# A fused state-space layer, forward and backward: long-convolution transforms in two matmul stages with a block transpose by VectorE, with their tables kept on chip

## The chip, the cores and the metric

The kernel runs on one core of a Trainium2 chip. The metric is the device time in microseconds (us) of one execution. A matmul engine (PE), a vector engine (DVE), an activation engine (ACT), a general engine (POOL) and a queueing engine (SP) run their own instruction streams, in order, and meet through semaphores; sixteen DMA engines move data between memory and the on-chip buffers. Matmul results land in PSUM, and from there ACT or DVE copies them to the ordinary on-chip memory (SBUF), where the next matmul can read them.

## The reference

Sizes are L = 2048 time steps, D = 512 channels, N = 128 states, F = 1792 hidden units, all in bf16.

```python
x  = A_u                                        # [1, L, D]
xn = layernorm(x)
# s = S4 convolution: a kernel K per channel, applied by FFT of length 2L
dt = exp(log_dt)[:, None]
P  = exp((dt * A)[:, :, None] * arange(L))      # A = A_re + i A_im, [D, N]
K  = einsum("dn,dnl,dn->dl", C, P, dt * B).real
s  = irfft(rfft(pad(xn.T, 2L)) * rfft(pad(K, 2L)))[:, :L].T + xn * Dskip
# gate
g  = silu(silu(xn @ w1) @ w2)
out = x + s * g
# result: out and the gradients of A_u, A_re, A_im, B_re, B_im, C_re, C_im,
#         log_dt, Dskip, w1, w2 for a given grad_out
```

The convolution needs a forward transform of xn, of K and of the gradient of s (called DS in the kernel), three products of spectra (xn with K for s; xn with DS for the gradient of K; K with DS for the gradient of xn) and three inverse transforms. Everything else is matrix products, the tables of powers that make K and take its gradient back, and elementwise work.

## The kernel before

Sequences of length 2048 lie in SBUF as 128 partitions by 16 tiles t by 512 channels; a transform runs over partitions and t. The program is written in six stages, with the order of all engines' instructions set by hand: generators that each yield after a piece of work are advanced against one another in loops.

**Stage 1** runs the layernorm, the FFN forward (`gen_ffn_fwd`, L554 to L639) and, between its pieces, two kinds of tables: the powers (`power_phases`) and the DFT tables (`dft_table_phases`, L375 to L431). The DFT table has 16 slices of 128 by 8 by 128. Nine are made by a fraction (`frac`, L271 and L272, DVE) and three passes of ACT (L399, L402, L403), seven more are mirrored from those by a matmul (L411) and an ACT copy (`tb_m`). Each slice is stored to memory in two forms, `TFd` for forward transforms and, transposed by PE or by the DMA (L420 to L427, copied at `tb_i`), `TId` for inverse ones.

**Stage 2** makes the convolution kernel K in four chunks (`chunk_tables` L807 makes table products on DVE, `chunk_K` L862 does the matmuls), transposes the power tables for later use (`gen_xt`, `gen_yt`: PE transposes, ACT copies L948 and L965, stores to `XTd` and `YTd`), and takes the spectrum of xn. The forward transform (`fwd_classes` L1004) is a dense matmul: the four residue classes of t each take 8 matmuls of 128x128x512 for a quarter kt of the spectrum, with a quarter of the table loaded from `TFd`; one ACT copy (L1013) for each class; then a radix-4 pass on DVE (`rad4`, L92 to L98: 2 full, 3 small and 2 full instructions). Spectra are stored to memory, `UXd` for xn. K itself is stored to `Kud` and loaded again in another order (`load_K`).

**Stage 3** (`gen_kt` L1244) takes K's spectrum in quarters (`fwd_eo`, matmuls at L1180, copies at L1182, with negated tables `TFn` made by ACT at L1145), stores it to `KXd`, multiplies it with xn's (`cplx_mul`, L106 to L109: two multiplications of 4096 elements a partition and two additions of 2048) and makes an inverse radix-4 pass.

**Stage 4** runs the inverse transform that gives s (`inv_mm` L1198; 16 matmuls of 128x128x512, L1204, for each pair of t, with table tiles `TIs` loaded from `TId`), scales it by ACT into `S_s` (L1455, two buffers), stores `S_s`, and makes the output gradient from it (`YOut`). Between the pairs stands the forward transform of DS (`DXform` L1390).

**Stage 5** runs the inverse transform for K's gradient dK, sums it in groups (L1639), stores the sums and loads them again as `Gt`; in its midst the products for the gradient of xn (`Prod` L1564). Then come the slabs (`Slabs` L1734), which take the gradient back through the power tables: for each step a product on DVE (`Gbd`, L1774), matmuls on quarter-width tiles (L1786), an ACT copy (`Vb`, L1788), products and sums on DVE (L1797 to L1800) and matmuls (L1815). Between slab steps stand the inverse transform for xn's gradient (`conv`, copied at L1700) and most of the gradient of w2 (`Dw2` L1594, 14 blocks of two halves, matmuls at L1611).

**Stage 6** is the backward FFN (L1872 to L1936), the gradients of w1 (L1996) and the last of the state-space parameters.

Of the kernel before, what the change touches and what calls it, by code (L numbers as in the profile page):

```python
# [14 lines left out]
P = 128  # L15
# [5 lines left out]
W = 512  # L21
TS = 2
# [65 lines left out]
def rad4(nc, out_e, out_o, A, t, inv):  # L88

    TT = nc.vector.tensor_tensor  # L90
    E, O = t[:, 0], t[:, 1]
    TT(out=t[:, :, :, 0, :].rearrange("p e c w -> p c e w"), in0=A[:, :, 0:2, :], in1=A[:, :, 2:4, :], op=ALU.add)  # L92
    TT(out=E[:, :, 1, :], in0=A[:, :, 0, :], in1=A[:, :, 2, :], op=ALU.subtract)
    i, j = (1, 3) if not inv else (3, 1)
    TT(out=O[:, 0, 1, :], in0=A[:, 1, i, :], in1=A[:, 1, j, :], op=ALU.subtract)
    TT(out=O[:, 1, 1, :], in0=A[:, 0, j, :], in1=A[:, 0, i, :], op=ALU.subtract)
    TT(out=out_e, in0=E, in1=O, op=ALU.add)
    TT(out=out_o, in0=E, in1=O, op=ALU.subtract)  # L98


def cplx_mul(nc, pool, a, b, conj_a=False):

    TT = nc.vector.tensor_tensor
    t1 = pool.tile([P, 2, 4, W], BF16, name="cm_t1", tag="cm_t1")
    t2 = pool.tile([P, 2, 4, W], BF16, name="cm_t2", tag="cm_t2")
    TT(out=t1[:], in0=b[:, :], in1=a[:, 0:1].to_broadcast([P, 2, 4, W]), op=ALU.mult)  # L106
    TT(out=t2[:], in0=b[:, :], in1=a[:, 1:2].to_broadcast([P, 2, 4, W]), op=ALU.mult)  # L107
    TT(out=t1[:, 0], in0=t1[:, 0], in1=t2[:, 1], op=ALU.add if conj_a else ALU.subtract)
    TT(out=t1[:, 1], in0=t1[:, 1], in1=t2[:, 0], op=ALU.subtract if conj_a else ALU.add)  # L109
    return t1  # L110
# [25 lines left out]
def kernel(ctx, tc, A_u, A_A_re, A_A_im, A_B_re, A_B_im, A_C_re, A_C_im, A_log_dt, A_Dskip, B_x, B_w1, B_w2, grad_out,  # L136
# [23 lines left out]
    k.TFd = dr.tile([4, P, T, 2, P], BF16, name="TFd")  # L160
    k.TId = dr.tile([P, T, 8, P], BF16, name="TId")
    XS = lambda nm: dr.tile([4, P, 2, 4, W], BF16, name=nm)
    k.UXd = XS("UXd"); k.DXd = XS("DXd"); k.KXd = XS("KXd")
# [6 lines left out]
    with tc.manual_schedule():  # L170
        stage_1(k)
        stage_3(k, *stage_2(k))
        stage_4(k)
        stage_5(k)
        stage_6(k)
# [198 lines left out]

def dft_table_phases(k, pool):  # L375

    nc = k.nc
    kv = pool.tile([P, 512], I32, name="kv", tag="tb_r")
    nc.gpsimd.iota(kv[:], pattern=[[4, 512]], base=1, channel_multiplier=0)
    kf = pool.tile([P, 512], F32, name="kf")  # L380
    nc.vector.tensor_copy(out=kf[:], in_=kv[:])
    lf = pool.tile([P, T], F32, name="lf")
    nc.vector.tensor_scalar(out=lf[:], in0=k.lvf[:], scalar1=1.0 / 8192.0, scalar2=None, op0=ALU.mult)
    nJ = pool.tile([P, P], BF16, name="nJ")
    nc.gpsimd.memset(nJ[:], 0.0)
    nc.gpsimd.affine_select(out=nJ[:], in_=nJ[:], compare_op=ALU.not_equal, fill=-1.0, base=1 - P, pattern=[[1, P]], channel_multiplier=1)
    st = {}
    nC = [0]

    def A(t):  # L390
        r = pool.tile([P, 512], I32, name="tb_r", tag="tb_r")
        v = pool.tile([P, 512], F32, name="tb_v", tag="tb_v", bufs=2)
        frac(nc, v[:], r[:], kf[:], lf[:, t:t + 1])
        st[t] = v

    def B(t):
        v = st[t]
        w = pool.tile([P, 512], F32, name="tb_w", tag="tb_w", bufs=2)
        nc.scalar.activation(out=w[:], in_=v[:], func=ACT.Abs)  # L399
        tf = pool.tile([P, 4, 2, P], BF16, name="tb_f", tag="tb_f", bufs=4)  # L400
        rr = lambda ap: ap.rearrange("p (a b) -> p a b", b=P)
        nc.scalar.activation(out=tf[:, :, 1, :], in_=rr(v[:]), func=ACT.Sin, scale=-2.0 * math.pi)  # L402
        nc.scalar.activation(out=tf[:, :, 0, :], in_=rr(w[:]), func=ACT.Sin, scale=-2.0 * math.pi, bias=k.halfpi[:])  # L403
        st[t] = tf

    def M(t):

        tf, tm = st[t], pool.tile([P, 4, 2, P], BF16, name="tb_m", tag="tb_f", bufs=4)
        ps = k.pd.tile([P, 2, 4, P], F32, name="ps_m", tag="pd")
        for c in range(2):  # L410
            nc.tensor.matmul(out=ps[:, c], lhsT=nJ[:], rhs=tf[:, :, 1 - c, :], start=True, stop=True)  # L411
        later(k, nc.scalar.copy, out=tm[:].rearrange("p a c b -> p c a b"), in_=ps[:])
        st[16 - t] = tm

    def C(t):
        tf = st[t]
        ti = pool.tile([P, 8, P], BF16, name="tb_i", tag="tb_i", bufs=2)
        nC[0] += 1
        if nC[0] % 2 == 0:
            nc.sync.dma_start_transpose(ti[:], tf[:].rearrange("p a c b -> p (a c b)"))  # L420
        nc.sync.dma_start(k.TFd[:, :, t].rearrange("a p c b -> p a c b"), tf[:])
        if nC[0] % 2:
            pt = k.ps.tile([P, 8, P], BF16, name="pt_ti", tag="pz", bufs=1)
            for i in range(8):
                nc.tensor.transpose(out=pt[:, i, :], in_=tf[:, i // 2, i % 2, :], identity=k.ident[:])
            later(k, nc.vector.tensor_copy, out=ti[:], in_=pt[:])
        st[t] = ti  # L427

    def S(t):
        nc.sync.dma_start(k.TId[:, t], st.pop(t)[:])  # L430
    return A, B, M, C, S  # L431
# [121 lines left out]
def gen_ffn_fwd(k, fs, W1, W2):  # L553
# [52 lines left out]
    for tc_ in range(4):  # L606
# [5 lines left out]
        for f0 in range(0, FT, 2):  # L612
# [13 lines left out]
            k.mid()  # L626
# [11 lines left out]
    for _ in prev:  # L638
        k.mid()  # L639
        yield  # L640


def ld_tf(k, kt, q=None):

    k.ntf += 1
    if k.ntf % 2:
        TFs = k.tfp.tile([P, DK, F], BF16, name="TFs", tag="W1")[:].rearrange("p k f -> p (k f)")[:, 0:T * 2 * P].rearrange("p (t c q) -> p t c q", t=T, c=2)
    else:
        TFs = k.tf2.tile([P, T, 2, P], BF16, name="TFs", tag="TFs")[:]
    (q or k.nc.sync).dma_start(TFs, k.TFd[kt])  # L650
    return TFs


def stage_1(k):
# [3 lines left out]
    k.ntf = 0  # L658
    k.tfp = ro.open("tfp"); fp = ro.open("fp"); fs = ro.open("fs", 2)
    pr = lo.open("pr")  # L660
    W1 = k.tfp.tile([P, DK, F], BF16, name="W1", tag="W1")
# [10 lines left out]
    tA, tB, tM, tC, tS = dft_table_phases(k, tab)  # L672
    s0, s1, s2, pX, pV, pA, pB, pC, pCC, pS = power_phases(k, pr, bs, k.par)
    at, mid, ready = {}, {}, []
# [88 lines left out]
def open_tables(k, b, q, fn=None):  # L763
# [480 lines left out]
def gen_kt(k, kq, K_b, UX):  # L1244
# [3 lines left out]
    st = {}  # L1248
# [792 lines left out]
```

## Time and profile before

| | us |
|---|---|
| runs shown (median) | 729.01 |
| lowest and highest of three | 724.71, 729.33 |
| span of the profiled execution | 724.9 |

The profiled execution's span lies at the low end of the runs, some 4 us under the median. A profile line gives the time of one execution: an engine's busy time, its share of the span and its number of instructions; in a table by stretches, each row is a stretch of the span with its length and each engine's busy time in it. The stage borders by the trace are about 155 to 168 (stage 1 ends), 288 (stage 3 begins), 413 (dK's inverse transform begins), 455 (it ends), 480 (first slab matmul) and 566 (stage 6 begins). The clock column is the granted clock of PE as a share of full speed. Line numbers such as L1204 are those of the kernel before.

### The profile page before, as it was taken

The page shows a single profiled execution, that of the slowest core. Times are in us where ns is not written, and L with a number is a line of the kernel's source. Part 1 is how long each engine was busy: PE and PEld are TensorE (multiplying, and loading weights), DVE is VectorE, ACT ScalarE, POOL GpSimd, SP SyncE. Part 2 cuts the span into 40 slices and gives each one's busy share as a digit, 9 for nine tenths or more (in the row PEclk, how much of TensorE's full clock was granted, in tenths as well). Part 3 has the DMA queues.
Part 4 walks back from the last instruction along what each step waited for, and adds up shares of the span by engine and source line. Part 5 has one row for each costly group of instructions (what it writes and reads, how often), then busy time and mean ns, then how long its engine had stood idle before and what let it go on. Part 6 is the DMA issues. An engine that isn't in the chain of part 4 may idle for free.

```text
span 724.9 us, 13172 instructions
## 1 busy us (share of the span) xinstructions
PE 643.6 (89%) x5068; PEld 327.8 (45%) x5068; DVE 608.0 (84%) x973; ACT 418.9 (58%) x521; POOL 91.5 (13%) x165
## 2 busy tenths in 40 slices
PE   5868879797978867999999899998999899999997
PEld 3524435343646745454444344443444344444453
DVE  7898989999999798899999999734669568899671
ACT  5998999974869955365534422254556534432331
POOL 2010000021110003000011102051223201200000
PEclk9989989999989999999999999999999999999999
DMA  9859889999998969599768798699879799989994
GB/s 262 277 179 298 272 272 278 321 288 365 296 334 267 284 186 283 210 378 378 267 232 308 280 343 310 170 303 330 272 251 364 148 314 335 347 220 219 240 260 146
DMA packets 175744, 200.91 MB, mean 277 GB/s; under 512 B 66973, under 2 KB 137508, under 8 KB 169762
## 3 DMA queue, kind: packets, MB, share of 16 engines
q1 hardware_dynamic: 157906, 136.30, 62.2%
q0 software_dynamic: 11408, 50.93, 19.8%
q10 hardware_dynamic: 6368, 12.86, 5.3%
q8 instruction: 39, 0.64, 0.3%
q14 instruction: 23, 0.19, 0.1%
HBM read 105.38 MB, written 83.38 MB: 260 GB/s over the span
## 4 chain that ended last, share of the span: by engine, by line
PE 39%; DVE 26%; DMA 13%; issue 10%; ACT 8%; SPq 2%; POOL 1%; ACTq 0%; DVEq 0%; POOLq 0%
PE ps_v L1204 8%; PE ps_w L1996 7%; PE ps_w L1611 5%; PE ps_f L1180 5%; PE ps_f L1012 3%; PE ps_dx L1909 2%; DVE dhT L1887 2%; DMA XTd<-XT 2%; DMA K_b<-Kud 2%; DMA YTl<-YTd 2%; DVE cm_t L106 2%; DVE cm_t L107 2%; DVE ak L76 2%; PE ps_g L1639 1%; DVE XYg L530 1%
## 5 line engine op out<-in xcount | busy, mean ns | idle before, releaser
L618 PE MATMUL ps_h<-XNT,W 128*128 128x512 bf16 x224 | 57.7, 405 | 19.6 <-ACT hs L621 19.6
L1204 PEld LDWEIGHTS <-TIs 128*128 128x128 bf16 x384 | 37.6, 99 | 50.7 <-issue 5.2
L1886 PE MATMUL ps_da<-DOT,W2T 128*128 128x512 bf16 x224 | 52.1, 379 | 3.4 <-DVE dhT L1887 3.4
L1909 PE MATMUL ps_dx<-W1T,dhT 128*128 128x512 bf16 x224 | 52.8, 379 | 2.1 <-DMA W1T<-in_B_w_dram 1.1
L591 PE MATMUL ps_o<-W,aT 128*128 128x512 bf16 x224 | 54.1, 390 | 0.4 <-DVE ak L76 0.4
L1611 PE MATMUL ps_w<-DO_all,AW 128*128 128x512 bf16 x224 | 52.0, 380 | 0.0
L1797 DVE TENSOR_TENSOR T<-Vb,YTl 128x2048 bf16<-128x2048 bf16 x16 | 19.6, 1224 | 37.7 <-ACT Vb L1788 37.5
L1996 PE MATMUL ps_w<-dhc,xn 128*128 128x448 bf16 x256 | 49.2, 352 | 0.0
L1918 ACT ACTIVATE dxn<-dxn,c,rstd 128x512 f32<-128x512 f32 x16 | 13.0, 814 | 62.5 <-DVE c L1917 62.5
L1180 PEld LDWEIGHTS <-TFs 128*128 128x128 bf16 x312 | 30.5, 99 | 40.9 <-issue 7.3
L1887 DVE TENSOR_TENSOR dhT<-ps_da,sd 128x1024 bf16<-128x1024 f32 x28 | 34.0, 1221 | 16.2 <-ACT sd L132 11.7
L948 ACT COPY XT<-pt_xt 128x1024 bf16<-128x1024 bf16 (+1 forms) x44 | 42.4, 1051 | 3.2 <-DMA XTd<-XT 3.1
L1180 PE MATMUL ps_f<-K_b,TFs 128*128 128x512 bf16 x168 | 40.7, 391 | 3.2 <-issue 2.4
L1788 ACT CAST Vb<-ps_V 128x1024 bf16<-128x1024 f32 x32 | 31.6, 1014 | 17.9 <-PE ps_V L1786 12.2
L618 PEld LDWEIGHTS <-W 128*128 128x128 bf16 x224 | 22.0, 102 | 43.5 <-issue 25.4
L1012 PE MATMUL ps_f<-xn,TFs 128*128 128x512 bf16 x128 | 32.7, 411 | 4.9 <-DMA TFs<-TFd 4.5
L591 PEld LDWEIGHTS <-aT 128*128 128x128 bf16 x224 | 22.6, 101 | 29.2 <-issue 4.9
L1996 PEld LDWEIGHTS <-xn 128*128 128x128 bf16 x256 | 25.0, 98 | 23.5
L1886 PEld LDWEIGHTS <-W2T 128*128 128x128 bf16 x224 | 21.7, 98 | 29.9 <-issue 4.9
L1909 PEld LDWEIGHTS <-dhT 128*128 128x128 bf16 x224 | 21.8, 98 | 29.2 <-issue 2.7
L1180 PE MATMUL ps_f<-DS,TFs 128*128 128x512 bf16 x144 | 33.2, 379 | 1.2 <-ACT S_s L1455 1.2
L946 PE MATMUL pt_xt<-ident_bfloat,X 128*128 128x128 bf16 x328 | 25.6, 227 | 8.1 <-ACT XT L948 6.3
(341 smaller groups left out, 1457.2 us busy)
## 6 DMA issues: line engine op xcount, KB each, us to landing
TIs<-TId SPq DMA_DIRECT2D x24, 512.0 KB, 4.4
XTd<-XT SPq DMA_DIRECT2D x20, 512.0 KB, 7.3
XTl<-XTd SPq DMA_DIRECT2D x15, 512.0 KB, 8.8
hTd<-hs SPq DMA_DIRECT2D x28, 256.0 KB, 3.1
akd<-ak SPq DMA_DIRECT2D x28, 256.0 KB, 3.1
UXl<-UXd POOLq DMA_DIRECT2D x7, 1024.0 KB, 8.7
dhd<-dhT SPq DMA_DIRECT2D x28, 256.0 KB, 4.5
XYd<-XYg SPq DMA_DIRECT2D x25, 256.0 KB, 3.1
```

The costliest lines, as they stand in the source:

```text
L591: nc.tensor.matmul(out=pso[:], lhsT=aT[:, ft, tt * P:(tt + 1) * P], rhs=W2[:, ft, :], start=(ft == 0), stop=(ft == FT - 1))
L618: nc.tensor.matmul(out=ps[:, j], lhsT=W1[:, dk, ft * P:(ft + 1) * P], rhs=XNT[:, dk], start=(dk == 0), stop=(dk == DK - 1))
L948: nc.scalar.copy(out=XT[:, j0:j0 + len(ks)], in_=pt[:, 0:len(ks)])
L1012: nc.tensor.matmul(out=ps[:, c, :], lhsT=TFs[:, t1 + 4 * j, c, :], rhs=src[:, t1 + 4 * j, :], start=(j == 0), stop=(j == 3))
L1180: nc.tensor.matmul(out=ps[:, c, :], lhsT=tab(j), rhs=at(t1 + 4 * j), start=(n == 0), stop=(n == 4 * len(terms) - 1))
L1204: nc.tensor.matmul(out=ps[:, j, :], lhsT=TIs[:, j, 2 * kt + c, :], rhs=B[kt][:, c, (t0 + j) % 4, :], start=(kt == 0 and c == 0), stop=(kt ...
L1611: nc.tensor.matmul(out=ps[:], lhsT=A[:, t, :], rhs=k.DO[:, t, :], start=(t == 0), stop=(t == T - 1))
L1788: nc.scalar.copy(out=self.V[i][:, g2], in_=ps[:].rearrange("p b c n -> p c b n"))
L1886: nc.tensor.matmul(out=ps[:, j], lhsT=self.W2T[:, ft // 2, dk, j * P:(j + 1) * P], rhs=self.DOT[tc_][:, dk], start=(dk == 0), stop=(dk == ...
L1887: nc.vector.tensor_tensor(out=self.dhT[:, f0:f0 + 2, :], in0=ps[:], in1=sd[:], op=ALU.mult)
L1909: nc.tensor.matmul(out=psx[:], lhsT=dhT[:, ft, t % 4 * P:(t % 4 + 1) * P], rhs=self.W1T[:, ft, :], start=(ft == 0), stop=(ft == FT - 1))
L1996: nc.tensor.matmul(out=ps[:], lhsT=k.xn[:, t, dk * P:(dk + 1) * P], rhs=ch[i][:, t, :], start=(t == 0), stop=(t == T - 1))
```

## The change

Each transform is now split in two. A table `TF` of 16 slices (made from `TI`, four table phases instead of nine, none of them stored) serves a first stage that works within each t, and a 16-point table `Wf` on the partitions serves a second stage that works across t. Between them the data has to change place: 32 x 32 blocks are transposed in place by DVE (`turn`). All of it runs on half of the channels at a time (H, 256 columns).

```diff
+HW = 256
...
-def rad4(nc, out_e, out_o, A, t, inv):
...
+def cplx_mul(k, a, b, conj_a=False):
...
+    t = k.mm.tile([P, 2, 2, 4, HW], BF16, name="cm_t2", tag="cm_t2")
...
+    TT(out=t, in0=b, in1=bc(1), op=ALU.mult)
+    TT(out=b, in0=b, in1=bc(0), op=ALU.mult)
+    TT(out=b[:, :, 0], in0=b[:, :, 0], in1=t[:, :, 1], op=ALU.add if conj_a else ALU.subtract)
+    TT(out=b[:, :, 1], in0=b[:, :, 1], in1=t[:, :, 0], op=ALU.subtract if conj_a else ALU.add)
+def fwd_first(k, A, src, H):
...
+    for q in range(8):
+        ps = k.pd.tile([P, 2, 2, HW], F32, name="ps_f", tag="pd")
+        for j in range(2):
+            for c in range(2):
+                nc.tensor.matmul(out=ps[:, j, c], lhsT=k.TF[:, 2 * q + j, c, :], rhs=src(2 * q + j)[:, d], start=True, stop=True)
+        nc.scalar.copy(out=A[:, 4 * q:4 * q + 4, :], in_=ps[:].rearrange("p j c d -> p (j c) d"))
+        yield
+def turn(k, A):
+    f = A[:].rearrange("p i d -> p (i d)").bitcast(F32).rearrange("p (i d) -> p d i", i=32)
+    for s in range(2):
+        v = f[:, 64 * s:64 * s + 64, :]
+        k.nc.vector.transpose(out=v, in_=v)
+def fwd_second(k, A, put):
...
+    for v in range(0, 16, 2):
+        ps = k.pd.tile([P, 2, 2, HW], F32, name="ps_s", tag="pd")
+        for j in range(2):
+            for c in range(2):
+                for h in range(2):
+                    nc.tensor.matmul(out=ps[64 * h:64 * h + 64, c, j], lhsT=k.Wf[:, c, 0:64], rhs=A[:, 2 * (v + j) + h, :], start=True, stop=True)
+        put(v, ps)
+        yield
+def inv_first(k, A, p, Y):
...
+    for v in range(8 * p, 8 * p + 8, 2):
+        ps = k.pd.tile([P, 2, 2, HW], F32, name="ps_i", tag="pd")
+        for j in range(2):
+            for c in range(2):
+                for h in range(2):
+                    z = slice(64 * h, 64 * h + 64)
+                    nc.tensor.matmul(out=ps[:, h, j], lhsT=k.Vi[z, c, :], rhs=Y[z, v % 8 // 4, c, v % 4 + j, :], start=(c == 0), stop=(c == 1))
+        nc.scalar.copy(out=A[:, 2 * v:2 * v + 4, :].rearrange("p (j h) d -> p h j d", h=2), in_=ps[:])
+        yield
...
-    k.TFd = dr.tile([4, P, T, 2, P], BF16, name="TFd")
-    k.TId = dr.tile([P, T, 8, P], BF16, name="TId")
...
+def inv_mm(k, ps, Z, t0):
+    for j in range(TS):
+        for H in range(2):
+            for c in range(2):
+                nc.tensor.matmul(out=ps[:, j, HW * H:HW * H + HW], lhsT=k.TI[:, t0 + j, c, :], rhs=Z[H][:, 2 * (t0 + j) + c, :], ...)
```

Each group of matmuls in `fwd_first`, `fwd_second` and `inv_first` has one copy by ACT behind it. A forward transform is, for each half, 8 groups, a turn and 8 groups; an inverse transform is 8 groups and a turn for each half, and then `inv_mm`, 8 matmuls of 256 columns for a pair of t instead of 16 of 512.

In stage 2 the spectra of xn and of DS both go through `spectrum`, four halves, one of them ahead of the chunk loop and three inside it, and are stored to `UXd` and `DXd` over POOL's queue:

```diff
+    def spec():
+        for src, dst in ((k.xn, k.UXd), (k.DS, k.DXd)):
+            for H in range(2):
...
+                yield from spectrum(k, uw, A[:].rearrange("p (i d) -> p i d", i=32), lambda t: src[:, t, :], dst, H, nc.gpsimd)
...
+    for _ in range(18):
+        next(fr)
+        tables_0(k)
```

In stage 3 K's spectrum is made into two tiles `KX` that stay on chip until stage 5. Stored spectra come back in four 1 MB parts (`ld_x`) on POOL's queue, into a ring of three buffers or a fourth of its own:

```diff
+        for n, _ in enumerate(fwd_second(k, A[H], put)):
+            if n == 3:
+                product(2 * H)
+        if H == 0:
+            product(1)
+    y.sil(0); y.sil(2)
+    back(0)
+    U[3] = ld_x(k, k.UXd, 3)
+    product(3)
+    y.pre(0); y.pre(2)
+    back(1)
```

In stage 5 the inverse transforms for dK and for xn's gradient have their first stages before the group sums and before the slabs; halves of w2's gradient stand between their groups, 20 of the 28, and the other 8 stay between the slab steps, where also the convolution's `inv_mm` stands. `B.dot(0)`, the first transposes of the backward FFN, moves behind the slabs.

```diff
+    def back(H, X, mul):
+        Z = k.fa.tile([P, 32, HW], BF16, name="FZ", tag="FA")
+        for p in range(2):
+            i = 2 * H + p
+            mul(i)
+            for n, _ in enumerate(inv_first(k, Z, p, X.pop(i)[:])):
+                if n % 2:
+                    dw2(1)
+        turn(k, Z)
+        return Z
...
+    Z = [back(0, D_, mul_d)]
+    Z.append(back(1, D_, mul_d))
+    dw2(4)
...
+    Z = [back(0, E_, mul_x)]
+    Z.append(back(1, E_, mul_x))
+    lo.close("sel", "ux")
+    ro.close("dkp", "kx")
     S = Slabs(k, lo.open("sw"))
```

More of the change, by code (lines that the diff above doesn't have):

```diff
@@ L406, in M @@
[L406 to L427, printed above, removed]
@@ L1723, in stage_5, with halves_of @@
             B.ld_g(0, nc.gpsimd); B.ld_g(1, nc.gpsimd)
[L1724 to L1729 removed]
     for _ in k.sl:
         pass
+    for _ in halves:
+        pass
+    B.dot(0)
+def halves_of(w2, ft):
+    yield from w2.run(ft)
+    yield
 class Slabs:
```

625 lines of the change are left out of this document (215 added, 410 removed).

## The prediction

> **What bounds the kernel now.** I read the engine totals and the chain of waits first, then the table by stretches (cut at the stage borders), then the timeline where stages meet, then groups by form and the DMA issues.
>
> ```profile
> PE 643.6 (89%) x5068; PEld 327.8 (45%) x5068; DVE 608.0 (84%) x973; ACT 418.9 (58%) x521; POOL 91.5 (13%) x165
> ...
> PE 39%; DVE 26%; DMA 13%; issue 10%; ACT 8%; SPq 2%; POOL 1%; ACTq 0%; DVEq 0%; POOLq 0%
> ```
>
> PE is busiest and leads the chain, but no stage is like the mean. Columns below: stretch, its length, busy us (and instructions) of PE, weight loads, DVE, ACT, POOL, then clock, DMA share, GB/s.
>
> ```profile
> 0.00:155.00 155.00, 120.39 (x783) 63.90 (x784) 140.17 (x316) 139.25 (x183) 12.26 (x26) 0.94 0.86 271
> ...
> 168.00:187.50 19.50, 15.68 (x68) 6.42 (x69) 18.30 (x29) 8.90 (x10) 3.06 (x5) 0.91 1.06 340
> 187.50:258.00 70.50, 58.49 (x1207) 42.94 (x1206) 65.87 (x109) 63.75 (x73) 7.88 (x13) 0.95 0.92 290
> 258.00:288.00 30.00, 20.74 (x442) 17.42 (x443) 27.26 (x29) 15.95 (x18) 7.97 (x16) 0.89 0.82 223
> 288.00:413.00 125.00, 119.33 (x578) 54.46 (x577) 119.72 (x134) 59.86 (x65) 13.45 (x27) 0.99 0.80 291
> 413.00:455.00 42.00, 40.96 (x179) 17.59 (x179) 41.41 (x40) 10.32 (x12) 5.99 (x9) 0.96 0.86 330
> 455.00:480.00 25.00, 25.00 (x123) 11.19 (x125) 13.17 (x14) 8.12 (x12) 7.19 (x9) 1.00 0.72 215
> 480.00:566.00 86.00, 81.09 (x896) 37.11 (x888) 55.97 (x77) 46.69 (x54) 18.60 (x35) 1.00 0.87 292
> 566.00:725.00 159.00, 149.67 (x755) 71.35 (x753) 113.43 (x199) 60.25 (x89) 12.81 (x24) 1.00 0.94 252
> ```
>
> Stage 1 (0–155) is filled by DVE and ACT together; stage 2's chunk loop (187.5–258) by ACT and DVE; stages 3 and 4 (288–413) and dK (413–455) by PE and DVE at once; the slabs (480–566) by PE. The change lightens PE everywhere and DVE somewhat, and loads ACT.
>
> **Prices.** All from these rows.
>
> ```profile
> 278.00 7.45 ACT L948 COPY XT<-pt_xt 128x1024 bf16<-128x1024 bf16 x8
> ...
> 307.38 2.29 DVE L106 TENSOR_TENSOR cm_t<-UXl,BY 128x4096 bf16<-128x4096 bf16 x1
> ...
> 314.30 1.23 DVE L92 TENSOR_TENSOR r_t<-cm_t 128x2048 bf16<-128x2048 bf16 x1
> ...
> 319.29 0.69 DVE L1190 TENSOR_TENSOR r_t<-BY 128x1024 bf16<-128x1024 bf16 x1
> ...
> 424.09 3.62 PE L1204 MATMUL ps_v<-BK,TIs 128*128 128x512 bf16 x16
> ...
> 283.19 3.74 PE L1125 MATMUL ps_dsk<-xn,DS 128*128 128x128 bf16 x64
> ...
> 484.56 1.06 PE L1786 MATMUL ps_V<-XTl,Gbd 128*32 128x256 bf16 x32
> ...
> 480.34 1.90 PE L1611 MATMUL ps_w<-DO_all,AW 128*128 128x512 bf16 x8
> ```
>
> An ACT copy of a 128x1024 PSUM tile is 7.45/8 = 0.93 us back to back. A complex product runs from 307.38 to 314.30: c = 6.9; the radix-4 pass behind it to 319.29: 5.0. Removing 17 of those frees 85 us of DVE. A matmul is about 0.22 us at 512 columns and 0.058 at 128, so about 0.11 at 256. Groups of eight on half-array tiles take 0.9 us one after the other, or 0.5 if two tiles run side by side; L1786's 32 matmuls of 256 columns on 32-wide tiles take 1.06 us, far under 32 x 0.11, so tiles do overlap. Either way a group stays under its copy's 0.93: ACT sets the rate of every new first or second stage. A half w2 product is 1.9.
>
> The StreamTranspose isn't in the trace. Nearest are 4-byte DVE passes:
>
> ```profile
> L530 DVE TENSOR_TENSOR XYg<-ex,b_w 128x1024 bf16<-128x1024 f32 x8 | 9.9, 1236 | 0.0
> ...
> L272 DVE SCALAR_TENSOR_TENSOR b_f<-tau,b_r 128x512 f32<-128x512 f32 x22 | 15.2, 692 | 0.8
> ```
>
> The slope is 0.544 us per 512, so 2048 words give 1.236 + 2 x 0.544 = 2.32, a turn T (two of them) 4.6. Bounds: 1.23 each (a 2048-element bf16 pass, L92) and twice the value, 4.6. I take 2.32, the same word size and one pass. The Trainium skill ("Vector Engine (DVE) Microarchitecture Reference", §3.8) has the 32x32 transpose sustain one element per cycle per lane; with 0.96 GHz ("VectorE: DVE Perf Modes") that is an estimate of 2.13, and the sum would come out about 2 us lower; no run here shows it yet.
>
> **1. Stage 1, -8.** Nine table phases become four; seven mirrors and all table spills go.
>
> ```profile
> L403 ACT ACTIVATE tb_f<-tb_w,halfpi 128x512 bf16<-128x512 f32 x9 | 6.7, 741 | 0.0
> ...
> L76 ACT CAST tb_m<-ps_m 128x1024 bf16<-128x1024 f32 x7 | 7.4, 1051 | 0.0
> ...
> L272 DVE SCALAR_TENSOR_TENSOR tb_v<-kf,lf,tb_r 128x512 f32<-128x512 f32 x9 | 6.8, 752 | 0.3
> ...
> L76 DVE COPY tb_i<-pt_ti 128x1024 bf16<-128x1024 bf16 x8 | 5.5, 686 | 4.1 <-PE pt_ti L425 4.1
> ...
> L271 DVE TENSOR_SCALAR tb_r<-kf,lf 128x512 int32<-128x512 f32 x9 | 4.3, 477 | 0.0
> ```
>
> Each phase is three ACT passes of about 0.7 and two DVE passes (0.752 + 0.477): 5 x 2.1 + 7.4 = 18 us off ACT, 5 x 1.23 + 5.5 = 11.6 off DVE. The new 16-point table adds about a dozen tiny DVE passes, two short ACT ones and a copy, some 3.5 of DVE at the start, where nothing covers them. DVE is the fuller engine by a hair, so it decides: 11.6 - 3.5 = 8. SP's queue loses the table stores between the FFN's stores. Bounds: -14 (ACT decides, less its own additions) and -3 (the matmuls of the FFN take over: PE is busy 120 of 155).
>
> **2. Head of stage 2, +8.5.** The first spectrum now has a turn in its middle. DVE's table products fill it until 184, so T queues behind them, and the first chunk matmul waits on PE behind the second stage.
>
> ```profile
> 183.39 0.68 DVE L835 TENSOR_TENSOR X<-m 128x1024 bf16<-128x1024 bf16 x1
> ...
> 187.48 1.33 PE L874 MATMUL ps_k<-X,CY 128*32 128x41 bf16 x64
> ```
>
> 184.1 + 4.6 + 8 x 0.93 = 196 against 187.5. Bounds +2 (T slips in between products) and +13 (the 32 transposes of the forward table and their four copies, 5 us, are in the way at the start as well).
>
> **3. Chunk loop, +31.** Both spectra, three halves of them, now have 48 copies here, where 10 of the old kind were; the last third shows ACT full:
>
> ```profile
> 237.00:258.00 21.00, 17.23 (x393) 12.99 (x390) 16.57 (x31) 21.00 (x25) 1.65 (x3) 1.00 0.92 271
> ```
>
> 38 x 0.93 = 35, less part of ACT's idle 6.8 in the loop: 70.5 becomes 102. Bounds +28 (all 6.8 absorbed) and +38 (ACT loses as much again as now to its partners). The added wait is of T for eight copies: DVE runs in order, so behind T stand the chunk's table products, PE's chunk matmuls wait for those, and ACT's next copies for PE; the three turns here are 14 us of DVE in the place of one radix-4 pass (5), and 65.9 + 9 doesn't fit into 70.5.
>
> **4. K's store and load, -1.** K goes out to memory and comes back as before:
>
> ```profile
> 287.93 1.02 PE L1180 MATMUL ps_f<-K_b,TFs 128*128 128x512 bf16 x4 [0.78 <-DMA K_b<-Kud]
> ```
>
> The first matmul of stage 3 waits for it in both kernels. DVE's three radix-4 passes and a product of this stretch (22 of its 27.3) go, but they stood beside this transfer; ACT's XT and YT copies stay beside it, and the three loads of UX that now come early are on POOL's queue. Bounds -6 and +4. So stage 3 starts at 287.9 - 8 + 8.5 + 31 - 1 = 318.
>
> **5. Stages 3 and 4, -33.** Counted from the start of stage 3: first stage 16 x 0.93 = 14.9; second stages to 29.8, with both turns of DVE under ACT's copies (cover gone: +4.6). c0 starts at 19.5 and c0, c1, c2 end at 40.2 on DVE, which ACT's next 8 copies don't outlast; T(Z0) to 44.8; c3, with UX's fourth part loaded into a freed buffer in 8.7, to 51.7; two G products 1.4; four copies 3.7; T(Z1): 62. Then stage 4:
>
> ```profile
> Sd<-S_s SPq DMA_DIRECT2D x8, 256.0 KB, 8.0
> ...
> UXl<-UXd POOLq DMA_DIRECT2D x7, 1024.0 KB, 8.7
> ...
> od<-o SPq DMA_DIRECT2D x8, 256.0 KB, 3.4
> ```
>
> PE needs 0.9 per pair of t instead of 3.6, but S_s has two buffers, each held 1.0 + 8.0: the stage takes about 3 x 9 + 3 = 30, beside which D's first product fits. SP, which carried the table tiles between these stores, has only the stores and the loads of co and cG left. 92 against 125. Bounds: stage 3 56 to 75 (c3's load early, or each hand-over between PE, ACT and DVE a microsecond), stage 4 20 to 33 (stores at 5, or at 9).
>
> **6. D back and dK, +26.** DVE's order: c1 6.9, copies 3.7, T 4.6, c2 and c3 13.8, copies 3.7, T 4.6: 37, and one load of 8.7 that waits for a buffer of the ring of three: 46. Twelve w2 halves, 23 us of PE, lie between the groups and run under it; if DVE were faster they would be late next. Then eight pairs of dK:
>
> ```profile
> L1639 PE MATMUL ps_g<-dK,gs_s 128*128 128x512 bf16 x48 | 12.0, 380 | 0.0
> ```
>
> PE's share of a pair is 0.9 of inverse and, with four small ones, 6.5 sums at 0.22, 1.4; a pair takes 2.45 with its hand-overs, over ACT's 1.0. DVE's three E products run beside it, 20.8 in 20. With the last copy and sums: 22. 68 against 42. Bounds 54 and 76: where the load comes early, and where two are late.
>
> **7. E back to the first slab matmul, +16.** Copies 7.4, T 4.6, c3 6.9, copies 3.7, T 4.6 = 27; the w2 halves hide on PE. Only then is the slabs' memory free:
>
> ```profile
> 470.55 1.92 ACT L1742 ACTIVATE XTl<-lvf 128x2048 f32<-128x2048 f32 x1
> ```
>
> Zeroing 1.9, a load of about 9 and the first products: 14, so 41 against 25. Bounds +8 and +22.
>
> **8. Slabs, -15.** Twenty of 28 w2 halves go to steps 6 and 7 (20 x 1.9 = 38 us of PE), and each convolution falls from 3.6 to 0.9 (-22), so PE's 81 becomes about 22 to 30 and DVE's rows decide:
>
> ```profile
> L1774 DVE TENSOR_TENSOR Gbd<-Gt,MK 128x512 bf16<-128x512 bf16 x32 | 20.5, 683 | 3.7 <-DMA Gt<-dKgd 3.7
> ...
> L1797 DVE TENSOR_TENSOR T<-Vb,YTl 128x2048 bf16<-128x2048 bf16 x16 | 19.6, 1224 | 37.7 <-ACT Vb L1788 37.5
> ...
> L1800 DVE TENSOR_TENSOR T<-Vb,YTl 128x1024 bf16<-128x1024 bf16 x32 | 20.6, 684 | 0.0
> ```
>
> 60.7 and 8 or more of start, joints and tail: 71 against 86. Bounds 64 and 80.
>
> **9. Stage 6, 0.** Its matmuls and passes are as before. B.dot(0) now stands before it, about +2, against the lighter DMA.
>
> **Sum.** -8 + 8.5 + 31 - 1 - 33 + 26 + 16 - 15 + 0 = +24.5 on the 724.9 of the profiled execution: 749.4. The three timed runs have a median of 729.0, some 4 above that span: 753.
>
> **Rivals.** *DMA relief, not slower.* Some 40 MB of table and K-spectrum traffic go and 6 MB of D's come, of 200.9. Place: the waits priced above at loaded latencies. If Sd's store lands in od's 3.4, stage 4 loses 12; UX and D loads at half, 8 in steps 6 and 7; K's load 4; stage 1 to its -14 end, 6: -30, so 723. It decides once S_s's store lands under 5 us. For it: the same 256 KB takes 3.4 in stage 1. Against it: stage 1's DMA share is no lower (0.86, against 0.80).
>
> *Slow transposes.* At 4.6 each, the six turns that lie open (one each in steps 2 and 7, two each in 5 and 6) cost 27 more: 780. For it: each instruction reads and writes words that lie 512 bytes apart, which no f32 row here does; against it: the f32 rows (L272, L530) already run at the slow word rate.
>
> *A cold PE.* After a gap the clock falls:
>
> ```profile
> 48.00:52.00 4.00, 0.50 (x2) 0.22 (x2) 3.90 (x8) 4.00 (x6) 1.60 (x1) 0.79 0.11 39
> 52.00:56.00 4.00, 4.00 (x11) 1.35 (x10) 3.86 (x9) 2.91 (x5) 0.00 (x0) 0.50 0.94 251
> ```
>
> PE was 0.5 of 4 us busy, and the next 4 us ran at 0.50. Steps 5 to 7 have such gaps at each T and c. If every group there takes double (1.8 instead of 0.9), ACT's 0.93 no longer sets it: about 16 groups on the path, +14: 767. The Trainium skill ("TensorE: Matmul & The Clock Gate", Part 1) states half rate after an idle window of about 3.4 us; this trace agrees with 0.50.
>
> That the half-array tiles don't overlap is no case of its own: 0.9 still fits under 0.93.
>
> **How the numbers follow.** Forecast 753 (own range 738 to 768, the steps' bounds added as independent): chance 0.50. DMA relief 0.24, slow transposes 0.15, cold PE 0.11. A measurement here tells about 1% from no change, 721.7 to 736.3. DMA relief spreads about 723: 0.13 faster, 0.09 same, 0.02 slower; the forecast gives 0.02 to same, the rest slower. So 0.13, 0.11, 0.76. The range 718 to 786 leaves out the lower third of DMA relief and the upper of slow transposes.
>
> **What would show it.** ACT full from about 190 to 290 shows step 3; stages 3 and 4 under 100 us with PE idle at each turn, step 5; transposes near 2.3, the price; slabs with DVE over 85% busy, step 8. The forecast is wrong if the chunk loop stays near 70 us (ACT had room), if transposes are off by double, or if Sd's stores land near 3.4.

## The result: 13.7% slower, 826.7 us against 726.9

Timed side by side, the changed kernel takes 826.73 us (median; 823.14 to 830.52) and the kernel before 726.86. The ratio is 1.1367, with a 95% interval from 1.1299 to 1.1435. The forecast was 753 with a range of 718 to 786. The sign was right and the size far off: 74 us over the forecast and 41 over the end of the range. The profiled execution has a span of 821.2 us.

The page of the kernel after: engine totals, then the two costliest groups of DVE, which are the turns (busy us, mean ns, idle before them and what ended it).

```profile
PE 579.7 (71%) x5192; PEld 334.6 (41%) x5232; DVE 596.5 (73%) x867; ACT 486.6 (59%) x587; POOL 97.5 (12%) x177
...
L120 DVE STREAM_TRANSPOSE FA<-FA 128x2048 f32<-128x2048 f32 x12 | 49.2, 4166 | 49.2 <-ACT FA L111 49.2
...
L120 DVE STREAM_TRANSPOSE FZ<-FZ 128x2048 f32<-128x2048 f32 x12 | 49.2, 4161 | 32.6 <-ACT FZ L146 32.6
```

PE is busy 64 us less, as the change intends, and no engine is now busy for more than 73% of the span. The kernel has become a row of waits. A transpose, half a turn, takes 4.17 us, not 2.32. The table by stretches of the kernel after, cut at its own stage borders:

```profile
0.00:163.50 163.50, 128.68 (x779) 66.84 (x794) 146.43 (x345) 135.18 (x178) 19.20 (x36) 0.96 0.68 224
163.50:196.70 33.20, 13.88 (x109) 9.20 (x109) 26.30 (x32) 17.65 (x19) 1.66 (x3) 0.67 0.41 124
196.70:326.00 129.30, 82.69 (x1667) 65.66 (x1666) 86.61 (x106) 99.79 (x111) 14.39 (x25) 0.82 0.59 185
326.00:367.00 41.00, 21.42 (x229) 19.54 (x220) 0.00 (x0) 18.86 (x21) 7.47 (x15) 0.63 0.92 275
367.00:442.00 75.00, 37.50 (x334) 24.87 (x331) 67.76 (x50) 48.29 (x51) 1.73 (x5) 0.72 0.11 36
442.00:476.00 34.00, 12.20 (x67) 7.77 (x66) 15.17 (x17) 12.57 (x13) 8.97 (x17) 0.60 0.72 258
476.00:528.00 52.00, 34.73 (x227) 16.96 (x232) 40.12 (x19) 19.77 (x24) 5.43 (x8) 0.81 0.72 253
528.00:546.00 18.00, 16.94 (x99) 9.27 (x98) 17.59 (x11) 8.40 (x10) 0.00 (x0) 1.00 0.13 39
546.00:589.00 43.00, 25.36 (x194) 12.11 (x201) 25.30 (x12) 20.98 (x25) 5.75 (x7) 0.83 0.43 119
589.00:663.00 74.00, 57.43 (x781) 31.12 (x786) 57.54 (x80) 45.28 (x52) 20.63 (x39) 0.87 0.93 266
663.00:821.00 158.00, 148.87 (x742) 71.29 (x752) 113.72 (x200) 59.84 (x88) 12.31 (x23) 1.00 0.93 248
```

To compare kernels I use landmarks that all of them have: first and last chunk matmul, first matmul on K_b, last `S_s` copy, last group sum of dK, first ps_V of the slabs, first ps_da of stage 6, end. The forecast's column is the kernel before plus the prediction's steps. The last three columns are experiments told below.

| stretch, us | before | forecast | after | half turn | no turn | no turn, XT pieces moved |
|---|---|---|---|---|---|---|
| start to first chunk matmul | 187.5 | 188.0 | 196.7 | 189.6 | 183.3 | 185.0 |
| chunk loop | 78.3 | 109.3 | 129.3 | 117.6 | 107.8 | 107.9 |
| to stage 3 (K's way out and back) | 21.0 | 20.0 | 41.1 | 40.6 | 41.2 | 20.0 |
| stages 3 and 4 | 129.4 | 96.4 | 109.0 | 97.0 | 88.6 | 100.6 |
| D back and dK | 39.0 | 65.0 | 69.9 | 68.9 | 64.8 | 62.5 |
| E back | 24.6 | 40.6 | 43.0 | 38.3 | 30.8 | 30.4 |
| slabs | 86.2 | 71.2 | 74.0 | 76.4 | 78.0 | 75.7 |
| stage 6 | 158.9 | 158.9 | 158.2 | 161.3 | 157.0 | 159.8 |
| span | 724.9 | 749.4 | 821.2 | 789.7 | 751.5 | 741.9 |

### The profile page after: what moved, and what is told of

The parts are those of the page before. It is cut to its first block, busy times and chain, and to the rows that moved or that the text cites. A ratio compares the mean times of both kernels' runs of the same rounds, so it can differ in the third digit from the quotient of the medians.

```text
span 821.2 us, 13331 instructions
## 1 busy us (share of the span) xinstructions
PE 579.7 (71%) x5192; PEld 334.6 (41%) x5232; DVE 596.5 (73%) x867; ACT 486.6 (59%) x587; POOL 97.5 (12%) x177
## 5 line engine op out<-in xcount | busy, mean ns | idle before, releaser
L120 DVE STREAM_TRANSPOSE FA<-FA 128x2048 f32<-128x2048 f32 x12 | 49.2, 4166 | 49.2 <-ACT FA L111 49.2
L146 ACT CAST FZ<-ps_i 128x1024 bf16<-128x1024 f32 x48 | 46.3, 1013 | 51.3 <-PE ps_i L145 49.5
L120 DVE STREAM_TRANSPOSE FZ<-FZ 128x2048 f32<-128x2048 f32 x12 | 49.2, 4161 | 32.6 <-ACT FZ L146 32.6
L131 PE MATMUL ps_s<-FA,Wf 128*64 128x256 bf16 x384 | 37.9, 338 | 47.9 <-DVE FA L120 36.3
L145 PE MATMUL ps_i<-XP,Vi 64*128 64x256 bf16 x384 | 34.5, 322 | 51.0 <-DVE XP L98 33.3
L1042 ACT CAST FX<-ps_s 128x1024 bf16<-128x1024 f32 x32 | 32.1, 1029 | 36.7 <-PE ps_s L131 25.4
L111 ACT CAST FA<-ps_f 128x1024 bf16<-128x1024 f32 x48 | 48.0, 1073 | 7.2 <-PE ps_f L110 7.1
L131 PEld LDWEIGHTS <-Wf 128*64 128x64 bf16 x384 | 25.4, 132 | 56.7 <-DVE FA L120 37.8
L145 PEld LDWEIGHTS <-Vi 64*128 64x128 bf16 x384 | 21.5, 107 | 66.3 <-DVE XP L98 38.4
L1153 PE MATMUL ps_v<-FZ,TI 128*128 128x256 bf16 x192 | 30.8, 316 | 23.7 <-ACT S_s L1319 13.8
L1633 PE MATMUL ps_V<-XTl,Gbd 128*32 128x256 bf16 x512 | 21.9, 306 | 22.1 <-DVE Gbd L1621 8.5
```

Of the source, the lines that this page charges most:

```text
L111: nc.scalar.copy(out=A[:, 4 * q:4 * q + 4, :], in_=ps[:].rearrange("p j c d -> p (j c) d"))
L120: k.nc.vector.transpose(out=v, in_=v)
L131: nc.tensor.matmul(out=ps[64 * h:64 * h + 64, c, j], lhsT=k.Wf[:, c, 0:64], rhs=A[:, 2 * (v + j) + h, :], start=True, stop=True)
L145: nc.tensor.matmul(out=ps[:, h, j], lhsT=k.Vi[z, c, :], rhs=Y[z, v % 8 // 4, c, v % 4 + j, :], start=(c == 0), stop=(c == 1))
L146: nc.scalar.copy(out=A[:, 2 * v:2 * v + 4, :].rearrange("p (j h) d -> p h j d", h=2), in_=ps[:])
```

## The experiments

The first four ask whether the size of the turn is all that was wrong, where that size comes from, and what stands in the gap ahead of stage 3. All edits are against the kernel after.

**Half a turn.**

```diff
-    for s in range(2):
+    for s in range(1):
```

> Each turn does only the first of its two transposes (the other half of the columns stays unturned), so that a turn costs about 4.2 us instead of 8.3, close to the 4.6 that the prediction put in its sum. If the size of that one term is what was wrong, the time comes out at the forecast, about 753 (the changed kernel 827 less 74). If the order of the queues is wrong as well, only the open part of twelve turns goes, some eight times 4.15: 33, so about 793, and the chunk loop and the gap ahead of stage 3 stay long (loop over 105 us, gap about 40).

Measured: 788.47 us, ratio 1.081 (1.071 to 1.091), 38 less. At about the price that the forecast had put in (4.2 for a turn, against 4.6), the kernel is still 40 us of span over the forecast. The table shows where: 20.6 in the gap ahead of stage 3, 8.3 in the chunk loop, and the other rows within 5.2 each, 11.4 together. The second reading held: the time, the loop and the gap all came out as it said.

**No turn.**

```diff
 def turn(k, A):
...
+    return
```

> The turns are left out altogether (the data stays in its old order). Size of the term alone: about 720, the prediction's sum without its open turns. Order as well: twice the effect of the half turn, 827 - 66 = 760; the gap between the last chunk matmul and stage 3 stays about 40 us, because no turn stands in it.

Measured: 753.09 us, ratio 1.0354 (1.0271 to 1.0437). The gap stayed at 41.2. Twelve turns are 24 x 4.17 = 100 us of DVE, and the span falls by 69.7, so 70% of that time lay open, which means that other work did not hide it; the prediction had six turns of twelve open. Even with the turns left out the changed kernel is slower than before. The two stretches from here, chunk loop and gap:

```profile
183.30:291.00 107.70, 79.79 (x1659) 63.97 (x1662) 59.89 (x96) 99.05 (x111) 14.31 (x25) 0.85 0.71 222
291.00:332.00 41.00, 19.58 (x232) 17.67 (x223) 0.00 (x0) 18.77 (x21) 7.49 (x15) 0.75 0.94 275
```

ACT is busy for 99 of 107.7 us: without turns its copies fill the loop. In the same stretch of the kernel before (187.5 to 265.8) it was busy for 65 of 78.3.

**Other forms of the turn.**

```diff
+    if k.nturn % 3 == 0:
+        f = flat.bitcast(F32).rearrange("p (d i) -> p d i", i=32)
...
+    elif k.nturn % 3 == 1:
+        f = flat.rearrange("p (d i) -> p d i", i=32)
...
+    else:
+        f = flat.rearrange("p (i d) -> p d i", i=32)
...
```

In this order: 4-byte words side by side, 2-byte elements side by side, 2-byte elements 512 bytes apart.

> A third of the turns each take another form over the same bytes: 4-byte words lying next to each other, 2-byte elements next to each other (twice as many), 2-byte elements 512 bytes apart. If the distance of 512 bytes between words makes the price, the first form falls from 4.17 us to about 2.1 to 2.3; if the word's size does, it stays at 4.17. By elements at one rate, the 2-byte forms take 4.2 for twice as many elements; by bytes, 4.2 as well, or 2.1 if 2-byte elements run faster. Only the durations of the forms are read here, since the data isn't turned as the kernel needs it.

The groups of one source line each: durations min/median/max in ns, first and last start.

```profile
L123 DVE STREAM_TRANSPOSE FA<-FA x4: 2266/2306/2315, 176.2 to 315.1; 128x2048 f32<-128x2048 f32 x4
...
L128 DVE STREAM_TRANSPOSE FA<-FA x4: 4402/4441/4445, 198.9 to 390.0; 128x4096 bf16<-128x4096 bf16 x4
...
L133 DVE STREAM_TRANSPOSE FA<-FA x4: 19144/19226/19299, 244.1 to 413.1; 128x4096 bf16<-128x4096 bf16 x4
```

Words side by side take 2.31 us, the prediction's 2.32. The same words 512 bytes apart take 4.17. It is the distance, then, not the word. Elements of 2 bytes run at the same rate by element side by side (4.44 for twice as many), and take 19.2 at 512 bytes' distance.

**The last XT and YT pieces among stage 3's groups.**

```diff
-    for g in sl:
+    for g in sl[:8]:
         next(g)
...
+        for n, _ in enumerate(fwd_first(k, A[H], at, H)):
+            if n % 2:
+                for g in rest:
+                    next(g)
+                    break
```

> The last seven of the fifteen XT and YT pieces (PE transposes and ACT copies of the last chunk) stand between the groups of stage 3's first stage again, as before the change, instead of ahead of it. If it is these copies that hold PE and ACT before stage 3 (they wait for buffers that the stores of XT free), the gap from the last chunk matmul to the first matmul of stage 3 falls from 41 us to 20 to 27 and the time by 12 to 20, to about 810. If K's own way out and back sets the gap, nothing changes: 827.

Measured: 815.03 us, ratio 1.1193 (1.1114 to 1.1272). Columns as in the table by stretches: gap, then stage 3.

```profile
327.00:346.00 19.00, 13.72 (x177) 12.49 (x171) 0.12 (x1) 12.81 (x14) 5.57 (x11) 0.82 0.87 218
346.00:431.00 85.00, 41.92 (x380) 28.73 (x379) 67.85 (x50) 54.46 (x59) 3.65 (x9) 0.74 0.34 115
```

The gap falls from 41 to 19, so these pieces held it, and stage 3 grows from 75 to 85, ACT's work in it from 48 to 54 us: half the gain is given back. What the pieces waited for is in the kernel after, in SP's timeline and then in ACT's (start us, us, instruction, idle before):

```profile
336.75 0.60 SPq L952 DMA_DIRECT2D K_b<-Kud  x1
338.78 20.73 SPq L1193 DMA_DIRECT2D XTd<-XT  x6
```

```profile
349.02 1.93 ACT L973 COPY XT<-pt_xt 128x1024 bf16<-128x1024 bf16 x2 [6.14 <-DMA XTd<-XT]
355.58 0.37 ACT L973 COPY XT<-pt_xt 128x256 bf16<-128x256 bf16 x1 [4.63 <-DMA XTd<-XT]
359.57 3.76 ACT L990 COPY YT<-pt_yt 128x1024 bf16<-128x1024 bf16 x4 [3.62 <-DMA XTd<-XT]
```

The program holds the stores of these pieces back, so that they stand behind K's loads in SP's queue: the last of SP's loads is at 336.75, the first store at 338.78, and ACT finds a freed buffer only at 349.02. Until then the four XT buffers are full. PE's first matmul of stage 3 (367.1) stands behind these transposes in its queue, and behind 64 matmuls at L1133 (5.9 us) that come after them.

**Table products ahead of the turn.**

```diff
-            if j in (4, 6, 8, 10, 12, 14):
+            if j < 6:
                 next(Tn)
```

> In the chunk loop the six pieces of the next chunk's table products go to DVE in the first six steps, ahead of the turn, instead of every second step from the fifth on, behind it. If DVE's queue is the cause (the turn waits there for eight ACT copies, 25 us in the first chunk, with the products queued behind it, and ACT and PE then wait for those), the loop falls from 129 us to about 110 and the time to about 808. If the loop is set by ACT's own work (100 us of copies) and the turn's wait only shows it, the loop stays above 122.

Measured: 829.73 us, ratio 1.1375 (1.1313 to 1.1436); the loop takes 130.0. My theory fell: DVE's long wait ahead of a turn holds up nobody who is late. ACT's own work doesn't set the loop either, since it is idle for 29.5 of 129.3 us. What matters comes behind the turn, as these rows of the kernel after show (the first turn in the loop, and ACT's first copy behind each of the three):

```profile
215.47 8.20 DVE L120 STREAM_TRANSPOSE FA<-FA 128x2048 f32<-128x2048 f32 x2 [25.63 <-ACT FA L111]
...
224.87 1.01 ACT L1042 CAST FX<-ps_s 128x1024 bf16<-128x1024 f32 x1 [6.78 <-issue]
...
266.74 1.01 ACT L1042 CAST FX<-ps_s 128x1024 bf16<-128x1024 f32 x1 [6.08 <-PE ps_s L131]
...
307.45 1.01 ACT L1042 CAST FX<-ps_s 128x1024 bf16<-128x1024 f32 x1 [6.35 <-PE ps_s L131]
```

ACT stands still while a turn runs, because the second stage's copies are next in its queue. The first row names no releaser, but it lies as the other two do: right behind the turn, and behind the matmuls that wait for the turn. The three waits are 19.2 us; the loop with turns takes 21.5 more than the loop without.

**Words side by side, as a working kernel.**

```diff
-    f = A[:].rearrange("p i d -> p (i d)").bitcast(F32).rearrange("p (i d) -> p d i", i=32)
+    f = A.rearrange("p d i e -> p (d i e)").bitcast(F32).rearrange("p (d i) -> p d i", i=32)
...
-        nc.scalar.copy(out=A[:, 4 * q:4 * q + 4, :], in_=ps[:].rearrange("p j c d -> p (j c) d"))
+        nc.scalar.copy(out=A[:, :, 4 * q:4 * q + 4, :].rearrange("p d i e -> p i d e"), in_=ps[:].rearrange("p j c (d e) -> p (j c) d e", e=2))
...
-                    nc.tensor.matmul(out=ps[64 * h:64 * h + 64, c, j], lhsT=k.Wf[:, c, 0:64], rhs=A[:, 2 * (v + j) + h, :], start=True, stop=True)
+                    nc.tensor.matmul(out=ps[64 * h:64 * h + 64, c, j], lhsT=k.Wf[:, c, 0:64], rhs=A[:, :, 2 * (v + j) + h, :], start=True, stop=True)
```

> The tile that is turned holds its 4-byte words side by side for one turn block (the ACT copies write them 128 bytes apart, the matmuls read them so), so that the turn runs on neighbouring words: 2.3 us instead of 4.17 for each transpose. If the copies and matmuls keep their time (0.93 and 0.11), this is worth as much as the half turn: 827 to about 788. If scattered 4-byte writes or reads are slower on ACT or PE, the 96 copies into such tiles or the 576 matmuls out of them take longer; at twice the copy's time the kernel would be slower than 827 by some 50.

Measured: 802.32 us, ratio 1.0997 (1.0953 to 1.1042): 24 less, not 38. Groups by source line, first of this kernel:

```profile
L120 DVE STREAM_TRANSPOSE FA<-FA x12: 2268/2286/2312, 175.4 to 370.4; 128x2048 f32<-128x2048 f32 x12
...
L131 PE MATMUL ps_s<-FA,Wf x384: 375/420/448, 179.9 to 384.8; 128*64 128x256 bf16 x192
...
L1153 PE MATMUL ps_v<-FZ,TI x192: 374/393/405, 413.5 to 636.2; 128*128 128x256 bf16 x192
...
504.14 1.89 PE L1153 MATMUL ps_v<-FZ,TI 128*128 128x256 bf16 x8
```

and of the kernel after (the last row of each is from PE's timeline: eight matmuls in a row):

```profile
L131 PE MATMUL ps_s<-FA,Wf x384: 269/297/423, 184.9 to 398.6; 128*64 128x256 bf16 x192
...
L1153 PE MATMUL ps_v<-FZ,TI x192: 269/273/422, 431.8 to 659.5; 128*128 128x256 bf16 x192
...
530.38 1.04 PE L1153 MATMUL ps_v<-FZ,TI 128*128 128x256 bf16 x8
```

Part of the price has moved to PE: a matmul that reads 256 columns as 4-byte pairs 128 bytes apart has a median of 393 to 420 ns instead of 273 to 297. In a row the difference is larger, because the records overlap there (eight of 273 ns take 1.04 us, not 2.18): eight strided ones take 1.89 us. ACT's copies into the tile hardly change (median 1.13 against 1.07 us). In the table's terms the loop is 120 and dK's stretch 23 instead of 18.

**PE kept busy.**

```diff
+def warm(k, n):
+    ps = k.pd.tile([P, 2, W], F32, name="ps_warm", tag="pd")
+    for i in range(n):
+        k.nc.tensor.matmul(out=ps[:, i % 2], lhsT=k.ident[:], rhs=k.xn[:, i % T, :], start=True, stop=True)
...
     back(0)
+    warm(k, 44)
```

> PE is kept busy in the five gaps of stages 3 to 5 in which it waits for a turn or a product, by 30 to 58 matmuls of 512 columns each into a PSUM tile that nobody reads (204 in all, fitted to the gaps at the full clock). If the low clock after the gaps (0.50 to 0.67 in 400 to 480) costs time, the forecast's cold rival, the time falls by 5 to 14. If ACT's and DVE's rates cover the slower matmuls, it stays within 3 of 827.

Measured: 823.77 us, ratio 1.1237 (1.1152 to 1.1322), and the profiled span is 821.4 against 821.2. A stretch of the kernel after in which PE has little to do, then the same stages (365 to 440 and 474 to 526) with PE kept busy:

```profile
420.00:440.00 20.00, 4.61 (x34) 2.74 (x35) 16.05 (x9) 3.85 (x4) 0.54 (x1) 0.50 0.13 39
```

```profile
365.00:440.00 75.00, 54.14 (x411) 32.34 (x411) 68.13 (x50) 48.20 (x51) 1.72 (x5) 0.86 0.10 35
...
474.00:526.00 52.00, 46.29 (x284) 22.30 (x290) 40.17 (x19) 19.64 (x24) 5.43 (x8) 0.91 0.71 254
```

The clock rises from 0.72 to 0.86 and from 0.81 to 0.91, and the stretches stay at 75 and 52 us. Only E back gets shorter (43.0 to 40.9), while the slabs take 79.7 against 74.0. The intervals of the two kernels overlap, so the second reading holds. The clock does fall in the gaps, as the cold rival said: to 0.50 from 420 to 440. The Trainium skill ("TensorE: Matmul & The Clock Gate", Part 1) has half rate for an idle PE, and that row agrees. But here it costs next to nothing; that ACT and DVE set the rate instead is what the unchanged stretches suggest.

**Spectrum loads later in stage 4.**

```diff
-        if t0 == 0:
+        if t0 == 4:
             D_[0] = ld_x(k, k.DXd, 0); U_[0] = ld_x(k, k.UXd, 0)
+        if t0 == 8:
             D_[1] = ld_x(k, k.DXd, 1); U_[1] = ld_x(k, k.UXd, 1, own=True)
```

> In stage 4 the four 1 MB loads of DS's and xn's spectra are issued two at t = 4 and two at t = 8 instead of all at t = 0, ahead of the co and cG loads on the same queue. If those loads hold co back (ACT waited 17.5 us for co in this stage), the stage falls from 34 us to about 22 and the time by 8 to 12; if then DS's first products come as much later, the gain is given back between the stage's end and dK's first copy (52 us now) and the time stays at 827.

Measured: 829.03 us, ratio 1.1377 (1.1323 to 1.1431). ACT's waits for co come to 17.1 us as against 17.5, at other places; the stage falls only from 34 to 31, and D's stretch to dK's first copy grows from 52 to 58. The longest waits, first in the kernel after, then in this one:

```profile
461.04 1.06 ACT L169 ACTIVATE co<-co 128x1024 bf16<-128x1024 bf16 x1 [9.22 <-DMA co<-od]
```

```profile
462.88 1.06 ACT L169 ACTIVATE co<-co 128x1024 bf16<-128x1024 bf16 x1 [6.51 <-DMA co<-od]
...
473.42 1.06 ACT L169 ACTIVATE co<-co 128x1024 bf16<-128x1024 bf16 x1 [8.57 <-DMA co<-od]
```

In the kernel after, the co load that ACT waits 9.2 us for was issued right behind the four large loads. Here ACT waits only 1.8 us for that load, and the long waits stand at two later ones, the first of them again issued right behind large loads. So the wait has moved with the loads: this order gains nothing, and whether the loads are what holds co back is not settled.

**A wider gap behind the turn, and DVE's share of the copies.**

```diff
-def spectrum(k, pool, A, src, dst, H, q):
+def spectrum(k, pool, A, src, dst, H, q, gap=7):
...
     turn(k, A)
-    yield
-    yield
+    for _ in range(gap):
+        yield
...
-            if j % 4 == 2:
+            if j % 2 == 0:
                 next(fr, None)
```

> In the chunk loop a half spectrum's second stage follows its turn after seven steps of the loop's other work instead of two (the spectrum takes two steps in every second round to make up for it). Without turns the loop took 108 us, with them 129: 7.2 us for each of the three. If they are open because ACT's copies of the second stage stand right behind them in its queue, the other copies now in between cover about 5 us of each, the loop falls to 113 to 119 and the time to about 814. If the turns' 25 us of DVE set the loop, it stays above 126.

Measured: 822.84 us, ratio 1.1262 (1.1175 to 1.1348). The loop falls from 129.3 to 122.5, a third of what the turns cost it, between the two readings. ACT's waits for the second stage's matmuls shrink from 19.2 us to 2.4, but its other waits, for PE and for stores that free its buffers, grow from 7.8 to 19 us; why they grow stays open. The interval overlaps that of the kernel after, so for the whole time the gain is not shown.

```diff
+        (nc.vector.tensor_copy if v % 4 and (dst is not k.UXd or H) else nc.scalar.copy)(out=X[:, :, v % 4:v % 4 + 2, :], in_=ps[:])
```

> As the run with the wider gap, and every second copy of the second stage in the loop (12 of 24) is made by DVE instead of ACT; DVE is idle for a third of the loop. If ACT's copies set the loop, as the prediction's term of 31 us has it, 12 x 0.93 = 11 more go: loop 103 to 109, time about 804. If DVE, waiting in order for these groups, makes its table products late, nothing more is gained or some lost.

Measured: 831.17 us, ratio 1.1363 (1.1279 to 1.1447). The loop in the kernel with the gap (the stretch is 1 us longer than by the landmarks), then with DVE's share:

```profile
199.00:322.50 123.50, 82.17 (x1675) 66.96 (x1675) 87.88 (x106) 99.62 (x112) 13.78 (x24) 0.82 0.62 192
```

```profile
194.80:329.30 134.50, 81.63 (x1659) 66.46 (x1661) 101.66 (x118) 88.00 (x98) 13.78 (x24) 0.80 0.56 177
```

ACT's work falls by 12 us and the loop grows by 12 (122.5 to 134.5): DVE's 14 us come in series, not beside ACT. So the second reading holds here. In the first chunk the table products at L843 start 22.1 us after the turn's start instead of 16.6; which late product costs what wasn't taken apart.

**All of it together, and what is left without turns.** The first joins four diffs shown above (words side by side, XT pieces, gap, DVE's share), the second two (no turn, XT pieces):

```diff
+    f = A.rearrange("p d i e -> p (d i e)").bitcast(F32).rearrange("p (d i) -> p d i", i=32)
...
+    for _ in range(gap):
+        yield
...
+        (nc.vector.tensor_copy if v % 4 and (dst is not k.UXd or H) else nc.scalar.copy)(out=X[:, :, v % 4:v % 4 + 2, :], in_=ps[:])
...
+    for g in sl[:8]:
```

> The edits that should each help, together: words side by side for the turn, the last XT and YT pieces among stage 3's groups, the wider gap and DVE's share of the loop's copies. If their gains add (24, 12, 12, 10), 827 becomes about 769, still 5% slower than before the change. If they overlap (a cheaper turn leaves less for the gap to hide), 780.

Measured: 803.99 us, ratio 1.0949 (1.0834 to 1.1064), so not shown to be better than the words side by side alone (1.0997). Both readings were too low. The loop, 120 there, is 132 here with DVE's share in it. No version with working turns comes near the kernel before.

```diff
 def turn(k, A):
...
+    return
...
+    for g in sl[:8]:
```

> The turns are left out, and the last XT and YT pieces stand among stage 3's groups. What the change costs apart from its turns and from that place should be left: 753 - 12 = 741, still slower than before by some 1.5%, with the chunk loop at 108 us against 78. If the copies that the place of the XT pieces moves into stage 3 are only in the way there because of the turns, more is gained: 731.

Measured: 744.86 us, ratio 1.0181 (1.0093 to 1.0269): near the first reading, 741, and still slower than before; whether by as much as 2% the interval leaves open. By the table's last column the loop costs 29.6 more than before, D and E back 29.3 more; stages 3 and 4 give 28.8 back and the slabs 10.5.

## Why the prediction was wrong

The forecast's span, 749.4, missed 821.2 by 71.8. Three steps failed and make up 60 of it: 31.5 for the price of a turn, 20.6 for the gap ahead of stage 3, 8.3 for the chunk loop.

**The price of a turn.** The term T = 4.6 was mis-sized: 8.3. The extrapolation was sound for the form it rested on (2.31 measured for words side by side, 2.32 forecast), but each instruction here steps 512 bytes, and that was put into a rival with a chance of 0.15 instead of into the sum. The quoted f32 rows say nothing of a step. The half turn puts the effect at 821.2 - 789.7 = 31.5 us. The slow-transposes rival, 780, had the right mechanism. It counted one open turn in step 7, where the step's own sum has two; with seven open turns it gives 32 us, close to the 31.5, and 785.

**Step 4, the gap ahead of stage 3.** It was costed at -1 because ACT's XT and YT copies were said to run beside K's transfer. They don't fit beside it: fifteen pieces need eight buffers, there are four, and the stores that would free them stand behind K's loads. Before the change, seven of the pieces stood inside stage 3. Moved, they cost 21 us in the gap, of which 10 come back in stage 3.

**Step 3, the chunk loop.** Its main term held: 38 more copies at 0.93 with ACT full. Without turns the loop grew by 29.5 with 34 more of ACT's work; forecast +31 and 35. What was missed is that turns are open there: ACT reaches the second stage's copies with two steps of other work in between, and waits 6.1 to 6.8 us at each of three. A wider gap took these waits away and brought back only a third of the time, so how to hide the turns there stays open. The prediction named the queue behind the turn on DVE, and that was the wrong queue: moving the products changed nothing.

**What held.** The start, with the half turn at nearly the price forecast, came out 1.6 us from the forecast, D back and dK 3.9 and E back 2.3; the products ahead of the first turn end at 176.7 instead of 184.0, close to step 1's -8. Stage 6 took 158.2 against 158.9. Stages 3 and 4 fit at the half turn (97.0 against 96.4), in part by luck: the step's own parts, 62 and 30, measure 63 and 34, and the table's forecast takes its 33 off a stretch 4.4 us longer than the 125 from which the step started.

The slabs took 74 against 71, and that is largely luck. Step 8 has PE fall from 81 us to 22 to 30 and DVE over 85% busy; measured are 57.4 us of PE and 57.5 of 74 (78%) for DVE. Of the twenty w2 halves that it took off PE, eight stood ahead of the slabs before the change as well, so only twelve left, 22 us and not 38; and the convolutions fell from 18.1 us in that stretch to 10.1, not by 22.

In stage 4 the store of `S_s` (to `Sd`) landed sooner,

```profile
Sd<-S_s SPq DMA_DIRECT2D x8, 256.0 KB, 4.6
```

4.6 us instead of 8.0, under the 5 us from which DMA relief was to decide, and yet ACT waited 17.5 us for co. DMA relief came in bytes (165 MB against 201), but no run here separates what it bought. The rest of the miss, 11.4 us spread over six rows at the half turn, stays unassigned.

## What to carry to other kernels

Price an instruction by its access pattern as well as by its size: where no row of the trace has the pattern, a price at the upper bound belongs into the sum until a run of it alone says otherwise. When a dense matmul is split in two, count the copies and passes between the halves first; here PE's work fell by 64 us, and the chain of ACT's copies, DVE's turn and ACT's copies behind it cost more; even with the turns left out the kernel was slower. And when a block of work is moved ahead of a stage, count its buffers against the stores that free them.

## What the runs showed of the hardware

DVE's 32x32 block transpose has a rate by element for neighbours (2.31 us for 2048 words, 4.44 for 4096 elements of 2 bytes a partition) and loses with a step of 512 bytes: 1.8 times for 4-byte words (4.17 us), 4.3 times for 2-byte elements (19.2 us). The Trainium skill's one element per cycle per lane ("Vector Engine (DVE) Microarchitecture Reference", §3.8) agrees with the first and not with the second, and the measurement decides. A matmul that reads pairs 128 bytes apart takes about 1.4 times as long as one that reads 256 neighbours (420 against 297 ns, median), and eight in a row 1.8 times as long (1.89 against 1.04 us).
